# Attention chunks issued in a periodic order written out by hand, on every engine, ahead of a routed feed-forward layer

## The chip, the cores and the metric

One core of a Trainium2 chip. The metric is the device time of one execution in microseconds (us), lower is better. Engines: PE (TensorE: matmuls and transposes, results in PSUM), PEld (its weight loads), DVE (VectorE), ACT (ScalarE), POOL (GpSimd, which also issues some of the DMAs), SP (SyncE, which here only issues DMAs). Each engine runs its instructions in the order of its own queue; an instruction waits there for the semaphores of what it reads, and for its output buffer to be free.

## What is computed

Decayed linear attention in blocks, for 4 batches, 8 heads, 768 positions, 64 channels, and then an expert layer in which every token goes to one of 8 experts of 384 tokens each:

```python
Dmask = where(rel >= 0, lam ** rel, 0)
for b in range(12):                                   # blocks of 64
    intra = einsum('bhic,bhjc->bhij', qb, kb) * Dmask
    intra = einsum('bhij,bhjd->bhid', intra, vb)
    inter = einsum('bhid,bhde->bhie', qb * lam_pow, kv_state)
    out[block] = intra + inter
    kv_state = lam ** 64 * kv_state + einsum('bhsd,bhse->bhde', kb * rev_pow, vb)
x = out as [3072 tokens, 512]
logits = x @ w_gate                                   # [3072, 8]
# greedy in order of falling logits: a token takes its best expert that has room (384 places)
out[mask_e] = relu(x[mask_e] @ w1[e]) @ w2[e]         # e = 0..7
```

## The kernel before

**Attention.** The tokens are worked through in 24 chunks of 128 positions (six to a batch), all 8 heads together. fp32 values are split into a high and a low 16-bit half, and a product is three matmuls (high-high, high-low, low-high). The steps of a chunk g, by the tiles they write (the names stand in the profile's rows and in the program):

- `load`: SP queues `qf`, `kf`, `vf` (256 KB each) from DRAM, three chunks ahead into four buffers.
- `prep`: `kp`, the two halves of k side by side: the high one by ACT (L964), the rest by DVE (L965; called `kpl` below). `vs` = v times a power of lam (POOL, L967), its halves `vh` (ACT, L970) and `vl` (POOL, L972).
- `turn_q`, `turn_k`: PE transposes q and kp (`Tq`, `Tk`, four transposes each); ACT and DVE split q into `qh` and `ql` (L996, L998); ACT copies `kT` (L983).
- `scores`: 24 matmuls into two PSUM banks `S0`, `S1` (`S`, L1009); for each bank ACT copies the high half `sp` (L1014), DVE writes the rest (L1015), POOL masks the triangle (L1018).
- `state`: 12 matmuls add k and v to a running state `stp` (L1068), split into `sth` (ACT) and `stl` (DVE, L1076). It is skipped in a batch's last chunk.
- `inter` and `intra`: the state product (24 matmuls, L1037) and the product with the masked scores (24 matmuls, L1049) add up in the PSUM tile `XL`; DVE scales it to `xs` (L1054). `XL` has one buffer, so a chunk's `inter` can't begin before the last reader of the chunk before is done.
- `turn_x`: SP stores `xs` to `x_dram`; PE transposes it (`Tx`, L1086), ACT and DVE split it into `xh` and `xl` (L1089, L1091).
- `gate`: 12 matmuls (L1105) write the chunk's logits into an unused corner of the **next** chunk's `XL`, and DVE copies them out (L1107). That copy is that tile's last reader.

**Order.** In the attention part a scheduler sets each engine's order from the program text and its own estimates. `run` gives the text: in step s it writes the steps of chunks s - 2 to s + 3 one after another and then calls `hook(s)`, which puts in the router's constants (s = 2), its first steps on logits that are there already (`ranges` in three parts at 19 to 21, `ranks` at 22 to 24: short DVE operations, but for one comparison of 1280 elements in each) and the first nine expert weights (`load_w`, from s = 20).

**Weights.** Each of 16 weights (1 MB in bf16, cast from 2 MB of fp32 on the way) is one DMA in POOL's queue. `load_w` is held back by a one-element DVE copy from a chunk's logits into the weight's tile, which the DMA must wait for.

**Routing and experts** (`_route_and_moe`) follow. There the text's order is kept on PE, POOL and DVE: a chain of short steps finds the places of all tokens; indirect DMAs in POOL's queue gather rows of `x_dram` into `xe`; PE does the two layers (`p`, L611 and L624), ACT copies `hT` and `oe` out of PSUM (`oe` has four buffers), and POOL's indirect DMAs scatter `oe` to the output. The remaining weights are queued between the gathers and scatters.

Of the kernel before, what the change touches and what calls it, by code (L numbers as in the profile page):

```python
# [23 lines left out]
class _Router:  # L24
# [11 lines left out]
    def constants(self):  # L36
# [8 lines left out]

        self.i_kt = iota("i_kt", [P, P, 24], [[1, P], [0, 24]], 1)
        self.i_j = iota("i_j", [P, 29, 24], [[1, 29], [0, 24]], 0)
        self.i_t = iota("i_t", [P, 24, 24], [[0, 24], [128, 24]], 0)
        self.i_p = iota("i_p", [P, 1], [[0, 1]], 0, 1, F32)
        self.i_e = iota("i_e", [P, 8], [[1, 8]], 0, 0, F32)  # L50
        self.i_e1 = iota("i_e1", [P, 8], [[1, 8]], 1, 0, F32)
        self.i_et = iota("i_et", [P, 24, 8], [[0, 24], [1, 8]], -8)
        self.i_g8 = iota("i_g8", [P, 9, 24], [[1, 9], [0, 24]], -8)
        self.gbase = iota("gbase", [1, 9, 24], [[384, 9], [0, 24]], 1, 0, F32)
        i_k = self.i_kt[:, :, 0]
        kvec = []
        for m, sc in enumerate((16384, 128, 1, 4096)):
            kx = rc.tile([P, P], BF16, name=f"kvec{m}")
            V.tensor_scalar(kx, i_k, float(sc), None, OP.mult)
            kvec.append(kx)  # L60
        self.kvec = kvec
        ones = {}
        for sc in (16384, 128, 64, 1):
# [3 lines left out]
        self.ones = ones  # L67
# [3 lines left out]
        slt = rc.tile([P, P], BF16, name="slt")  # L71
        G.memset(slt, 0.0)
        G.affine_select(out=slt, in_=slt, compare_op=OP.is_ge, fill=1.0, base=0,
                        pattern=[[-1, P]], channel_multiplier=1)
        self.slt = slt
        sltm = rc.tile([P, P], BF16, name="sltm")
        V.tensor_scalar(sltm, slt, 1.0, None, OP.subtract)
        self.sltm = sltm
# [19 lines left out]
        G.memset(self.ind2[:, 64:128, :], 0.0)  # L98
# [811 lines left out]
class _Attn:  # L910


    def __init__(self, ctx, tc, q, k, v, lam, w_gate, identf, logits, x_dram):
# [4 lines left out]
        P = 128  # L918
        cp = ctx.enter_context(tc.tile_pool(name="ac", bufs=1))
        self.io = ctx.enter_context(tc.tile_pool(name="aio", bufs=4))  # L920
        self.wk = ctx.enter_context(tc.tile_pool(name="awk", bufs=2))
        self.pt = ctx.enter_context(tc.tile_pool(name="apt", bufs=3, space=bass.MemoryType.PSUM))
        self.p1 = ctx.enter_context(tc.tile_pool(name="ap1", bufs=1, space=bass.MemoryType.PSUM))

        lam_sb = cp.tile([P, 8], F32, name="lam_sb")
        nc.sync.dma_start(out=lam_sb, in_=lam[None, :].to_broadcast([P, 8]))
        n_idx = cp.tile([P, 6], F32, name="n_idx")
        nc.gpsimd.iota(n_idx, pattern=[[P, 6]], base=1, channel_multiplier=1,
                       allow_small_or_imprecise_dtypes=True)
        loglam = cp.tile([P, 8], F32, name="loglam")  # L930
# [4 lines left out]
        lampow = cp.tile([P, 6, 8], F32, name="lampow")  # L935
        lamneg = cp.tile([P, 6, 8], F32, name="lamneg")
        nc.scalar.activation(lamneg, nlog, ACT.Exp, scale=-1.0)  # L937
        nc.scalar.activation(lampow, nlog, ACT.Exp)
        self.lampow, self.lamneg = lampow, lamneg
        wgf = cp.tile([P, 4, 8], F32, name="wgf")  # L940
        nc.sync.dma_start(out=wgf, in_=w_gate.rearrange("(c p) e -> p c e", p=P))
        wgh = cp.tile([P, 4, 8], BF16, name="wgh")
        nc.vector.tensor_copy(wgh, wgf)
        wgl = cp.tile([P, 4, 8], BF16, name="wgl")
        nc.vector.tensor_tensor(wgl, wgf, wgh, OP.subtract)
        self.wgh, self.wgl = wgh, wgl

    def load(self, g):
        nc, P = self.nc, 128
        b, t = divmod(g, 6)  # L950
        ts = slice(t * P, (t + 1) * P)
        qf = self.io.tile([P, 8, 64], F32, tag="qf")
        nc.sync.dma_start(out=qf, in_=self.q[b, :, ts, :].rearrange("h p d -> p h d"))
        kf = self.io.tile([P, 8, 64], F32, tag="kf")
        nc.sync.dma_start(out=kf, in_=self.k[b, :, ts, :].rearrange("h p d -> p h d"))
        vf = self.io.tile([P, 8, 64], F32, tag="vf")
        nc.sync.dma_start(out=vf, in_=self.v[b, :, ts, :].rearrange("h p d -> p h d"))
        return qf, kf, vf

    def prep(self, g, qf, kf, vf):  # L960
        nc, P = self.nc, 128
        t = g % 6
        kp = self.wk.tile([P, 8, 64, 2], F16, tag="kp", bufs=4)
        nc.scalar.copy(kp[:, :, :, 1], kf)  # L964
        nc.vector.tensor_tensor(kp[:, :, :, 0], kf, kp[:, :, :, 1], OP.subtract)  # L965
        vs = self.wk.tile([P, 8, 64], F32, tag="vs")
        nc.gpsimd.tensor_tensor(vs, vf, self.lamneg[:, t, :, None].to_broadcast([P, 8, 64]),  # L967
                                OP.mult)
        vh = self.wk.tile([P, 8, 64], BF16, tag="vh", bufs=5)
        nc.scalar.copy(vh, vs)  # L970
        vl = self.wk.tile([P, 8, 64], BF16, tag="vl", bufs=5)
        nc.gpsimd.tensor_tensor(vl, vs, vh, OP.subtract)  # L972
        d = dict(kp=kp, vh=vh, vl=vl, qf=qf)
        return d

    def turn_k(self, g, d):
        nc, P = self.nc, 128
        kT_ps = self.pt.tile([P, 4, P], F32, tag="T", name="kT_ps")
        kpf = d["kp"].rearrange("p h d s -> p (h d s)").bitcast(F32)
        for hp in range(4):  # L980
            nc.tensor.transpose(kT_ps[:, hp, :], kpf[:, hp * P : (hp + 1) * P], self.identf)  # L981
        kT = self.wk.tile([P, 4, P], F32, tag="kT")
# [4 lines left out]
    def turn_q(self, g, d):  # L987
        nc, P = self.nc, 128
        qf = d["qf"]
        qT_ps = self.pt.tile([P, 4, P], F32, tag="T", name="qT_ps")  # L990
        for hp in range(4):
            nc.tensor.transpose(qT_ps[:, hp, :],  # L992
                                qf[:, 2 * hp : 2 * hp + 2, :].rearrange("p h d -> p (h d)"),
                                self.identf)
        qh = self.wk.tile([P, 4, P], F16, tag="qh", bufs=3)
        nc.scalar.copy(qh, qT_ps)  # L996
        ql = self.wk.tile([P, 4, P], F16, tag="ql", bufs=3)
        nc.vector.tensor_tensor(ql, qT_ps, qh, OP.subtract)  # L998
        d["qh"], d["ql"] = qh, ql

    def scores(self, g, d):
        nc, P = self.nc, 128
        kT, qh, ql = d["kT"], d["qh"], d["ql"]
        S = [self.p1.tile([P, 4, P], F32, tag=f"S{a}", name=f"S{a}") for a in range(2)]
        for hp in range(4):
            for i, (ks, qq) in enumerate(((1, qh), (1, ql), (0, qh))):
# [51 lines left out]
    def state(self, g, d):  # L1058
        nc, P = self.nc, 128
        if g % 6 == 5:  # L1060
            return None
# [75 lines left out]
def kernel(  # L1137
# [23 lines left out]
    with ExitStack() as actx:  # L1161
        attn = _Attn(actx, tc, q, k, v, lam, moe_w_gate, identf, logits, x_dram)

        def hook(s):
            if s == 2:
                router.constants()
# [45 lines left out]
```

## Time and profile before

| | |
|---|---|
| time, median of 3 runs | 325.89 us (323.84 to 327.85) |
| the profiled execution's own time | 328.17 us |
| its span, first to last instruction | 326.4 us |
| mean granted TensorE clock | 0.876 |
| busy share of the span: PE, PEld, DVE, ACT, POOL | 77%, 60%, 58%, 51%, 52% |
| first copy of `kp` (L964), last copy of logits (L1107) | at 6.5 us, at 177.6 to 177.9 us |
| DMA | 52.05 MB moved, mean 159 GB/s |

Times in the rows are us from the span's start. A row of a timeline has start, length, engine, line, operation, output<-inputs, shape, count, and in brackets the idle time before it and what ended it. Busy PE time includes the tail in which a matmul drains, so matmuls that follow closely start more often than their lengths say. The clock column of a stretch is the share of the TensorE clock that was granted.

### The profile page before, as it was taken

Reading aid. Unit: us, or ns where it says so; the run is one execution under the profiler, and the core shown is the slowest. Engines: PE = TensorE matmul, PEld = TensorE weight load, DVE = VectorE, ACT = ScalarE, POOL = GpSimd, SP = SyncE. Lnnn points to the kernel's source line nnn. Section 1 sums busy time; section 2 is a strip of 40 time slices with the busy share of each in tenths; the row PEclk is TensorE's granted clock in tenths of the full one; section 3 lists DMA queues with packets and bytes.
Section 4 is the critical chain, followed back from the end, with each engine's and each line's share of the span. In section 5 each row is a group of like instructions: output and inputs, shape, how many; then the busy total and the mean of one; then the engine's idle time right before and its main releaser. Section 6 shows DMA issues by size and latency. Waiting matters only on the chain.

```text
span 326.4 us, 8813 instructions
## 1 busy us (share of the span) xinstructions
PE 249.9 (77%) x3538; PEld 197.1 (60%) x3551; DVE 190.7 (58%) x597; ACT 167.4 (51%) x297; POOL 169.9 (52%) x189
## 2 busy tenths in 40 slices
PE   1778778777979779788856535899809999899980
PEld 0657657666867668677655424577506666677750
DVE  4568758776696766878987578577705773000000
ACT  3757658676675766766621000255223555556650
POOL 5967646656375563755754708644345217445221
PEclk9999999979797797979895555599967999999996
DMA  8998768866797666973999999999999214434211
GB/s 140 218 166 189 165 151 187 174 140 133 176 194 148 131 137 165 195 155 67 209 222 236 209 209 209 186 204 211 223 224 265 74 66 103 115 94 99 80 69 37
DMA packets 96977, 52.05 MB, mean 159 GB/s; under 512 B 76961, under 2 KB 88225, under 8 KB 96929
## 3 DMA queue, kind: packets, MB, share of 16 engines
q0 software_dynamic: 17920, 26.22, 41.0%
q1 hardware_dynamic: 79008, 25.19, 36.0%
q8 instruction: 30, 0.49, 0.6%
q14 instruction: 19, 0.15, 0.2%
HBM read 58.74 MB, written 12.58 MB: 218 GB/s over the span
## 4 chain that ended last, share of the span: by engine, by line
PE 34%; DVE 20%; POOL 12%; issue 12%; DMA 11%; ACT 8%; SPq 0%; POOLq 0%; DVEq 0%; ACTq 0%
PE p L611 7%; PE p L624 7%; DMA out_dram<-oe,perm 6%; DVE sp L1015 4%; POOL vs L967 4%; ACT sp L1014 4%; DVE xs L1054 4%; POOL sp L1018 4%; DMA xe<-x_dram,perm 4%; PE S L1009 3%; PE XL L1105 2%; PE XL L1049 2%; DVE kp L965 2%; PE kT_ps L981 2%; PE xT_ps L1086 2%
## 5 line engine op out<-in xcount | busy, mean ns | idle before, releaser
L611 PE MATMUL p<-xeT,w 128*128 128x256 bf16 (+1 forms) x512 | 51.7, 255 | 11.5 <-ACT hT L616 8.8
L1018 POOL TENSOR_SCALAR_AFFINE_SELECT sp<-sp 128x512 f32<-128x512 f32 x48 | 36.3, 762 | 44.5 <-DVE sp L1015 35.6
L611 PEld LDWEIGHTS <-w 128*128 128x128 bf16 x512 | 40.1, 100 | 20.0 <-issue 13.6
L630 POOL DMA_INDIRECT out_dram<-oe,perm x24 | 24.1, 1004 | 45.2 <-ACT oe L629 35.7
L624 PE MATMUL p<-w,hT 128*128 128x512 bf16 x179 | 43.3, 379 | 0.8
L1015 DVE TENSOR_TENSOR sp<-S,sp 128x512 bf16<-128x512 f32 x48 | 33.3, 734 | 17.9 <-ACT sp L1014 17.9
L1014 ACT CAST sp<-S 128x512 bf16<-128x512 f32 x48 | 32.5, 739 | 20.8 <-PE S L1009 20.6
L580 POOL DMA_INDIRECT xe<-x_dram,perm x24 | 26.5, 1102 | 31.0 <-DMA w<-in_moe_w_dram 11.4
L616 ACT ACTIVATE hT<-p 128x512 bf16<-128x512 f32 (+1 forms) x64 | 31.3, 491 | 18.9 <-PE p L611 15.1
L972 POOL TENSOR_TENSOR vl<-vs,vh 128x512 bf16<-128x512 f32 x24 | 28.3, 1181 | 13.5 <-ACT vh L970 12.9
L629 ACT COPY oe<-p 128x512 f32<-128x512 f32 x24 | 14.1, 586 | 36.5 <-PE p L624 24.9
L1009 PE MATMUL S<-qh,kT 64*128 64x128 f16 x384 | 30.0, 229 | 1.5 <-DVE sp L1015 1.5
L1049 PE MATMUL XL<-vh,sp 128*128 128x64 bf16 x384 | 24.3, 198 | 7.6 <-POOL sp L1018 7.3
L967 POOL TENSOR_TENSOR vs<-vf,lamneg 128x512 f32<-128x512 f32 x24 | 27.3, 1136 | 3.8 <-ACT lamneg L937 3.8
L598 ACT COPY xeT<-pt 128x1024 bf16<-128x1024 bf16 (+1 forms) x16 | 12.8, 798 | 30.4 <-PE pt L594 30.3
L1049 PEld LDWEIGHTS <-sp 128*128 128x128 bf16 x576 | 21.5, 101 | 10.6 <-POOL sp L1018 9.8
L624 PEld LDWEIGHTS <-hT 128*128 128x128 bf16 x192 | 17.0, 97 | 16.6 <-issue 0.3
L981 PE MATMUL kT_ps<-identf,kp 128*128 128x128 f32 x96 | 18.2, 320 | 9.7 <-DVE kp L965 8.5
L1009 PEld LDWEIGHTS <-kT 64*128 64x128 f16 x576 | 20.4, 99 | 7.0 <-issue 2.3
L1009 PE MATMUL S<-ql,kT 64*128 64x128 f16 x192 | 23.1, 227 | 0.0
L992 PE MATMUL qT_ps<-identf,qf 128*128 128x128 f32 x96 | 18.3, 318 | 5.4 <-DMA qf<-in_q_dram 5.4
L970 ACT CAST vh<-vs 128x512 bf16<-128x512 f32 x24 | 14.9, 620 | 14.4 <-POOL vs L967 14.4
(256 smaller groups left out, 582.9 us busy)
## 6 DMA issues: line engine op xcount, KB each, us to landing
w<-in_moe_w_dram POOLq DMA_DIRECT2D x16, 1024.0 KB, 14.5
qf<-in_q_dram SPq DMA_DIRECT2D x24, 256.0 KB, 3.6
kf<-in_k_dram SPq DMA_DIRECT2D x24, 256.0 KB, 4.6
vf<-in_v_dram SPq DMA_DIRECT2D x24, 256.0 KB, 4.9
x_dram<-xs SPq DMA_DIRECT2D x24, 256.0 KB, 2.2
xe<-x_dram,perm POOLq DMA_INDIRECT x24, 7.0
out_dram<-oe,perm POOLq DMA_INDIRECT x24, 3.3
lam_sb<-in_lam_dram SPq DMA_DIRECT2D x1, 4.0 KB, 2.9
```

What stands on the lines that cost most here:

```text
L580: nc.gpsimd.indirect_dma_start(out=xe[:, c, :], out_offset=None, in_=self.x_dram, in_offset=bass.IndirectOffsetOnAxis(ap=pm, axis=0), boun ...
L611: nc.tensor.matmul(p1[:, f, 0:n, :], self.w1t[e][:, kc, fc * P : (fc + 1) * P], j["xeT"][:, kc, 0:n, :], start=(kc == 0), stop=(kc == 3), ...
L616: nc.scalar.activation(hT[:, fp, :, 0:n, :], p1[:, :, 0:n, :], ACT.Relu)
L624: nc.tensor.matmul(p2, j["hT"][:, kc // 2, kc % 2, c, :], self.w2t[e][:, kc, :], start=(kc == 0), stop=(kc == 7))
L967: nc.gpsimd.tensor_tensor(vs, vf, self.lamneg[:, t, :, None].to_broadcast([P, 8, 64]), OP.mult)
L972: nc.gpsimd.tensor_tensor(vl, vs, vh, OP.subtract)
L981: nc.tensor.transpose(kT_ps[:, hp, :], kpf[:, hp * P : (hp + 1) * P], self.identf)
L1009: nc.tensor.matmul(S[a][:, hp, :], kT[r, hp, :, ks], qq[r, hp, :], start=(i == 0), stop=(i == 2))
L1014: nc.scalar.copy(s[:, :, :, 1], S[a])
L1015: nc.vector.tensor_tensor(s[:, :, :, 0], S[a], s[:, :, :, 1], OP.subtract)
L1018: nc.gpsimd.affine_select(out=sf, in_=sf, compare_op=OP.is_ge, fill=0.0, base=0, pattern=[[0, 4], [1, P]], channel_multiplier=-1)
L1049: nc.tensor.matmul(X[a][:, hp, :], sp[a][:, hp, :, ss], vv[:, h, :], start=(first and hp == 0 and i == 0), stop=(i == 2), skip_group_check ...
```

## The change

The steps of a chunk become methods of their own with the same operations on the same data, but for two: `kpl` moves from DVE to POOL, and the copy `kT` from ACT to DVE. The order of all engines in the attention part is now that of the text (`tc.manual_schedule()`), and the text is made by sorting: operation `name` of chunk g stands at `g * PERIOD + AT[name]`, the router's steps and the weights at numbers of their own. The numbers only sort; nothing waits for a time. A chunk's operations reach over more than four periods, so that in one period S stands for chunk g - 1, G for g - 4, I and X for g - 2, and so on. Names: kph, kpl halves of kp; h0, h1 / l0, l1 / m0, m1 copy, rest and mask of the two score banks; I state product, X score product, G gate, lg its copy, xo the store; lq, lk, lv the loads of chunk g + 4.

```diff
+    PERIOD = 5.30
+    AT = dict(kph=0.00, kpl=0.90, Tq=1.33, vs=2.14, Tk=2.24, qh=3.12, vh=3.74, kT=4.23, ql=4.91,
+              vl=4.98, S=5.82, h1=6.88, h0=7.65, l1=8.00, l0=8.76, m1=8.84, ST=9.08, m0=9.60,
+              sth=11.42, stl=12.39, I=13.36, X=15.17, xs=16.23, Tx=19.16, xh=20.28, xl=22.24,
+              G=23.05, lg=23.70, lq=2.0, lk=2.2, lv=3.4, xo=17.0)
+    AHEAD = 4
...
+    def run(self, others):
+        self.begin()          # lam, then kf before qf and vf, for four chunks
+        work = list(others)
+        work.append((-2.0, self.powers))
+        for g in range(24):
+            for name, at in self.AT.items():
+                t = g * self.PERIOD + at
...
+                work.append((t, lambda f=getattr(self, name), n=g: f(n)))
+        for _, f in sorted(work, key=lambda w: w[0]):
+            f()
...
-        nc.vector.tensor_tensor(kp[:, :, :, 0], kf, kp[:, :, :, 1], OP.subtract)
+        self.nc.gpsimd.tensor_tensor(d["kp"][:, :, :, 0], d["kf"], d["kp"][:, :, :, 1],
+                                     OP.subtract)
...
-        nc.scalar.copy(kT, kT_ps)
+        self.nc.vector.tensor_copy(kT, d["kTp"])
...
-    moe = _Moe(ctx, tc, identb, x_dram, moe_w1, moe_w2, out, 10)
+    moe = _Moe(ctx, tc, identb, x_dram, moe_w1, moe_w2, out, 8)
...
-            for m in {20: (0,), 21: (1, 2), 22: (3,), 23: (4,), 24: (5, 6), 25: (7, 8)}.get(s, ()):
-                moe.load_w(m, logits[0:1, s - 2, 0:1])
+        others = [(t, lambda: next(steps, None))
+                  for t in (-3.0, -1.0, 3.5, 132.3, 135.0)]
+        others += [(t, lambda i=i: router.ranges(logits, 18, attn.ps, "qT", i))
+                   for i, t in enumerate((127.5, 128.0, 128.6))]
+        others += [(t, lambda a=a, b=b: router.ranks(logits, a, b))
+                   for t, a, b in ((129.0, 0, 10), (133.6, 10, 20), (140.9, 20, 23))]
+        others += [(t, lambda m=m: moe.load_w(m)) for m, t in
+                   enumerate((125.3, 126.3, 128.1, 129.0, 130.0, 133.5, 134.0, 134.5))]
+        with tc.manual_schedule():
+            attn.run(others)
...
-    fi = _route_and_moe(ctx, tc, logits, router, moe, range(9, 16))
+    fi = _route_and_moe(ctx, tc, logits, router, moe, range(8, 16))
```

The router's constants become five pieces (the `steps` above), two of them near the end; the clearing of a table (`ind2`) moves from POOL to DVE. The three transposes get PSUM banks of their own (`qT`, `kT`, `xT`, one each) instead of three shared ones; `S0`, `S1`, `XL` and `stp` keep one buffer each. Some SBUF rings change by one buffer (`kp` 4 to 3, `vh` and `vl` 5 to 4, `qh` and `ql` 3 to 4, `sp` 2 to 3, `sth`, `stl`, `xs` 2 to 3).

What this does to the queues, at three places. On PE, where the gate stands, in the middle of attention. Before, the matmuls of L1009 around it are one chunk's scores:

```order
L1009 MATMUL S_852<-qh,kT 128x128
L1105 LDWEIGHTS xh
L1105 MATMUL XL<-wgh,xh 128x8
...
L1105 LDWEIGHTS xl
L1105 MATMUL XL<-wgh,xl 128x8
L1009 LDWEIGHTS kT
L1009 MATMUL S_853<-qh,kT 128x128
```

Now (L1056 scores, L1019 `Tq`, L1182 gate, L1038 `Tk`, L1103 state product, L1159 `Tx`):

```order
L1056 LDWEIGHTS kT
L1056 MATMUL S_866<-qh,kT 128x128
L1019 MATMUL qT_ps<-identf,qf 128x128 x4
L1182 LDWEIGHTS xh
...
L1182 MATMUL XL<-wgh,xl 128x8
L1038 MATMUL kT_ps<-identf,kp 128x128 x4
L1103 LDWEIGHTS qh
...
L1159 MATMUL xT_ps<-identf,xs 128x128 x4
L1114 LDWEIGHTS sp_747
```

The last five score matmuls of a chunk stood behind the gate; now all 24 stand ahead of it, and `Tk`, the state product, `Tx`, the state and the score product of other chunks follow.

On POOL, one chunk's worth in the middle of attention. Before (L967 `vs`, L972 `vl`, AFFINE_SELECT the masks):

```order
L1018 AFFINE_SELECT sp_878<-sp_878 128x512
L967 TENSOR_TENSOR vs<-vf,lamneg 128x512
L1018 AFFINE_SELECT sp_882<-sp_882 128x512
L972 TENSOR_TENSOR vl<-vs,vh 128x512
```

Now:

```order
L996 TENSOR_TENSOR kp<-kf,kp 128x512
L1002 TENSOR_TENSOR vs<-vf,lamneg 128x512
L1083 AFFINE_SELECT sp_592<-sp_592 128x512
L1083 AFFINE_SELECT sp_619<-sp_619 128x512
L1013 TENSOR_TENSOR vl<-vs,vh 128x512
```

A fifth operation, the rest of `kp`, comes in, and the two masks stand together.

On DVE, near the end of attention, behind `ql` of chunk 23 (now; L1141 `stl`, L146 and L159 the first and the long operation of the first `ranks`, L1187 the logits of chunk 20, L1072 the score rests of chunk 23, L1147 `xs`, L1170 `xl`):

```order
L137 TENSOR_SCALAR sc<-sc 128x1
L1141 TENSOR_TENSOR stl<-stp,sth 128x512
L146 TENSOR_REDUCE r_v<-logits 128x10
...
L159 TENSOR_TENSOR ind_160<-q_3581,i_kt 128x128x10
...
L1187 COPY logits<-XL 128x8
L1072 TENSOR_TENSOR sp_3572<-S_3523,sp_3572 128x512
L1072 TENSOR_TENSOR sp_3605<-S_3522,sp_3605 128x512
L1147 TENSOR_TENSOR xs<-XL,lampow 128x2x4x64
L1170 TENSOR_TENSOR xl<-xT_ps,xh 128x512
```

The whole first `ranks` (12 operations) now stands in one piece ahead of the logits of chunk 20 and of the last chunk's score rests, and the second one, likewise, ahead of the logits of chunk 21. On POOL the first weight stands behind `vs` of chunk 23, the others between the last masks, eight in all, none with a copy from the logits ahead of it.

More of the change, by code (lines that the diff above doesn't have):

```diff
@@ L44, in iota @@
             return a
[L46 to L62, printed above, removed]
+        self.ones = ones = {}
         for sc in (16384, 128, 64, 1):
@@ L984, in turn_k, with S @@
         d["kT"] = kT.rearrange("p c j -> p (c j)").bitcast(F16).rearrange(
             "p (c j s) -> p c j s", c=4, s=2)
[L987 to L990, printed above, removed]
+    def S(self, g):
+        d = self.d[g]
+        d["S"] = [self.ps.tile([128, 4, 128], F32, tag=f"S{a}", name=f"S{a}") for a in range(2)]
+        d["sp"] = [None, None]
         for hp in range(4):
[L992 to L999, printed above, removed]
@@ L1044, in intra, with X @@
+    def X(self, g):
+        d = self.d[g]
         first = g % 6 == 0
[L1045 removed]
+        for a in (1, 0):
             for hp in range(4):
                 h = 2 * hp + a
[L1048 to L1051 removed]
```

388 lines of the change are left out of this document (209 added, 179 removed).

## The prediction

> **What bounds the kernel now.** I read the stage table first (one row per stretch of the span: its length, then busy time and instructions of PE, weight loads, DVE, ACT and POOL, the granted clock, the DMA share and GB/s), then the chain of waits inside the first stage, then what PE waits for in the last.
>
> ```profile
> 12.00:143.80 131.80, 105.87 (x1936) 90.33 (x1935) 92.58 (x157) 88.51 (x155) 78.22 (x86) 0.92 0.77 165
> 143.80:177.90 34.10, 24.81 (x481) 20.86 (x480) 30.14 (x87) 16.00 (x28) 19.99 (x23) 0.84 0.93 176
> 177.90:207.10 29.20, 15.14 (x166) 12.89 (x166) 20.77 (x83) 1.01 (x1) 16.05 (x17) 0.50 1.17 209
> 207.10:235.40 28.30, 28.11 (x250) 19.65 (x253) 20.57 (x120) 12.44 (x19) 14.77 (x15) 0.92 1.19 205
> ```
>
> Attention fills the first two stretches; the last logits are copied at 177.9. In the first no engine is full: DVE 70%, ACT 67%, POOL 59%, PE 80% (its drains counted). So order and waits set its pace. The second, with the routing's first steps mixed in, is DVE's (88%). Then come 29.2 us of routing, the experts, a hole of 8.8 us on PE, and the rest of the experts to the span's end at 326.4, 82.2 us.
>
> The chain of waits over one chunk (start, length, what) shows why a chunk takes 7.0 us there (34.89 to 41.90) on idle engines:
>
> ```profile
> 34.89 0.74 ACT sp L1014
> 35.73 0.76 DVE sp L1015
> 36.55 0.64 POOL sp L1018
> 37.19 1.46 POOL vs L967
> 40.41 0.69 DVE xs L1054
> 41.14 0.44 PE XL L1105 x12
> 41.59 0.29 PE S L1009 x5
> 41.90 0.75 ACT sp L1014
> ```
>
> Copy, rest and mask of a chunk's scores, then its product, `xs`, then the gate's 12 matmuls, and only behind these the last five score matmuls of the next chunk, which the next copy needs: a loop from one chunk to the next.
>
> The hole later is a queue:
>
> ```profile
> 222.41 20.56 DMA out_dram<-oe,perm
> 244.21 1.01 PE L611 MATMUL p<-xeT,w 128*128 128x256 bf16 x4 [8.78 <-ACT hT L616]
> ```
>
> An output scatter issued at 222.4 lands at 243.0, behind weights in POOL's DMA queue; ACT's copies wait for its buffer, and PE for ACT.
>
> **The change, part by part.** *The loop.* In the new order all 24 score matmuls stand ahead of the gate, and a chunk's product comes two places later, so the loop above is cut. What can bound a chunk next are the sums of each engine and the remaining loops.
>
> POOL now has, per chunk, `vs`, `vl`, two masks and `kpl` (min/median/max in ns; the last row gives mean ns after its busy time):
>
> ```profile
> L1018 POOL TENSOR_SCALAR_AFFINE_SELECT sp<-sp x48: 624/635/1236, 18.0 to 169.6; 128x512 f32<-128x512 f32 x48
> L967 POOL TENSOR_TENSOR vs<-vf,lamneg x24: 1031/1043/1514, 8.9 to 160.3; 128x512 f32<-128x512 f32 x24
> L972 POOL TENSOR_TENSOR vl<-vs,vh x24: 1146/1158/1698, 12.2 to 167.3; 128x512 bf16<-128x512 f32 x24
> L965 DVE TENSOR_TENSOR kp<-kf,kp x24: 714/766/1216, 7.3 to 158.4; 128x512 f16<-128x512 f32 x24
> L187 POOL TENSOR_TENSOR r_zp<-Z,H 128x192 f16<-128x192 f32 x1 | 0.6, 605 | 0.1
> ```
>
> No row shows `kpl` on POOL. The same subtraction with a dense output, `vl`, took 1.16; the one POOL row with a strided f16 output took 605 ns for 192 elements, 1.61 for 512 if all of it grows. So POOL needs 2 x 0.635 + 1.043 + 1.158 = 3.47, plus 1.16 to 1.61: 4.63 to 5.08 us.
>
> By the Trainium skill (GPSIMD Engine Reference, 4.1 Engine selection) an elementwise operation of two inputs is about 2x slower on GpSimd and belongs on VectorE, which speaks against this move: as an estimate from it, twice the 766 ns is 1.53 and POOL's sum 5.0. The trace's like pair, 1158 against 766, is 1.5x.
>
> DVE back to back starts an operation every 0.59 us, not every 0.68, and its copy of logits is short:
>
> ```profile
> 31.62 0.68 DVE L1091 TENSOR_TENSOR xl<-xT_ps,xh 128x512 bf16<-128x512 f32 x1
> 32.21 0.68 DVE L998 TENSOR_TENSOR ql<-qT_ps,qh 128x512 f16<-128x512 f32 x1
> 34.62 0.17 DVE L1107 COPY logits<-XL 128x8 f32<-128x8 f32 x1 [0.53 <-PE XL L1105]
> ```
>
> DVE gives `kpl` away and takes `kT`: two rests of scores, `kT`, `ql`, `xs`, `xl`, most chunks `stl`, seven starts of 0.6 and 0.17: 4.4 us. ACT loses `kT`. DMA moves the same 1.05 MB a chunk; at 5.1 us a chunk that is 206 GB/s, a share of 0.77 x 206/165 = 0.96, where the rows above reach 1.19; a share of 1.0 is reached at 4.9 a chunk.
>
> The longest loop left runs product, `xs`, `xl`, gate, logits' copy, state product, `Tx`, state, product, since the copy must free the bank for the next chunk. Its PE pieces at full clock, by starts:
>
> ```profile
> 35.04 0.20 PE L1037 MATMUL XL<-sth,qh 64*128 64x64 bf16 x2
> 35.50 0.55 PE L1086 MATMUL xT_ps<-identf,xs 128*128 128x128 f32 x3
> 35.88 0.60 PE L992 MATMUL qT_ps<-identf,qf 128*128 128x128 f32 x4
> 36.31 0.22 PE L1068 MATMUL stp<-vh,kp 128*128 128x128 bf16 x1
> 36.93 0.22 PE L1068 MATMUL stp<-vh,kp 128*128 128x128 bf16 x1
> 112.86 0.71 PE XL L1049 x24
> ```
>
> State product 0.46 (35.04 to 35.50), transposes 0.38 for three, so 0.50 for four, state 0.68 (12 starts, the first and last shown), product 0.71. With `xs` 0.60, `xl` 0.68, gate 0.44, copy 0.17 and some 0.18 of gaps: 4.4 us.
>
> So a chunk costs at least 4.63 (POOL), and 5.08 with the dear `kpl`. POOL and DVE also stretch each other: the `vs` of 1.46 in the chain, 0.42 over its median, lay beside the `kpl` that now leaves DVE. If this stays, 5.08 + 0.42 = 5.5. These sums have no waits, and each of POOL's five operations follows another engine, so I take 5.1, the upper end without stretching; 4.6 and 5.5 stay for the range.
>
> *The start.* `kf` is now queued first:
>
> ```profile
> 2.25 4.23 DMA kf<-in_k_dram
> ```
>
> Issued 1 us earlier, it lets chunk 0 begin at about 5.7 instead of 6.5. 24 chunks of 5.1 end at 128.1.
>
> *The tail.* On DVE `ranges` and the first `ranks` now stand ahead of the logits of chunk 20 and the rests of chunk 23, the second `ranks` ahead of the logits of chunk 21. In the stretch of 87 DVE instructions and 30.14 us above, 35 belong to chunks and 7 are the one-element copies that held the weights back. The new tail keeps 14 of the 35, none of the 7, and adds the mask `sltm`: 30.1 - 21 x 0.6 - 7 x 0.1 + 1.0 + a second `ae` of about 1 = 19 us. Three times DVE then waits for PE with little beside it: a round of state product, `Tx` and product is 0.46 + 0.50 + 0.71 = 1.7 at full clock and 3.0 at half (rows further down); two rounds, the first partly beside chunk 23's rests, and a gate of 0.44 make about 5. The tail is 24 us, and the last logits come at 152.1 instead of 177.9.
>
> *Weights and experts.* The program from routing on is unchanged, except that eight weights are queued ahead instead of nine. Their pace:
>
> ```profile
> 178.39 1.64 POOL L562 DMA_DIRECT2D w<-in_moe_w_dram x2 [1.48 <-DVE r_v L143]
> DMA to landing us min/median/max: 20.6/22.7/24.7
> 202.28 1.77 POOL L562 DMA_DIRECT2D w<-in_moe_w_dram x2
> ```
>
> The two issued at 178.4 and 179.2 land at 199.0 and 203.9, 5 us apart, so the queue was still full when the next two came, 24.4 us after the last logits. Eight queued from 126 (behind chunk 23's `vs`, 5.7 + 23 x 5.1 + 3.2) are through by about 171 (5 to begin, 8 x 5), 19 after the last logits; then the queue runs empty. The next two, at 24.4, find nothing ahead, where they had 1.6 us of weights and four gathers of some 1.8; so they, and the scatters behind them, land about 3.4 sooner counted from the last logits. Routing (29.2) is a chain on DVE and PE and stays; PE's first 28.3 us stay; the hole shrinks to 5.4; 82.2 follow. 145.1 in all.
>
> *Sum.* 152.1 + 145.1 = 297.2 of span, against 326.4. The profiled execution's own time is 328.2, its median of runs 325.9; 29.2 off gives 299.0 for a like execution and **297** for the median.
>
> **The clock.** Rows of 3.41 us, with PE's busy time, instructions and granted clock:
>
> ```profile
> 64.58:68.00 3.42, 1.69 (x42) 1.00 0.40 78
> 68.00:71.41 3.41, 3.41 (x44) 0.50 0.97 237
> 78.24:81.65 3.41, 2.28 (x56) 1.00 0.25 48
> 81.65:85.06 3.41, 3.41 (x38) 0.50 1.04 244
> ```
>
> A row half busy is followed by one at half clock; so is the one of 2.28, two thirds busy. At the present pace PE is busy 80% of the first stretch; with chunks a quarter shorter and the same matmuls it is busy nearly always, and I count no half rows before the tail. The Trainium skill (TensorE: Matmul & The Clock Gate, What's actually happening) wants an idle window of about 3.4 us before the clock halves. Its halves and its window length agree, but 2.28 us busy was enough here, so the trace decides: by the page the clock rival below could not occur, by the rows it can.
>
> **Rivals.** *The clock turns the loop into the bound.* At half clock:
>
> ```profile
> 68.43 0.76 PE XL L1037 x24
> 174.51 0.97 PE xT_ps L1086 x4
> 70.44 1.21 PE stp L1068 x12
> 161.27 1.28 PE XL L1049 x24
> ```
>
> The loop grows by 0.30 + 0.47 + 0.53 + 0.57, and `Tk` (as long as `Tx`), hidden beside the logits' copy at full clock, by some 0.6: 6.9 us a chunk, 297 + 24 x 1.8 = 340. It is slower than before from 6.3 a chunk, that is if three quarters of the rows are halved; it feeds on the waits of a fixed order. Against it: full rows end it.
>
> *The order does not cut the waits*: one late instruction holds its whole engine, and a chunk stays near 6.0 to 6.4, 319 to 328, no change. For it: every engine now waits in order. Against: the loop of the chain is gone by the program.
>
> *POOL is the bound with stretching*, 5.5 a chunk: 307.
>
> **How the numbers follow.** Forecast (4.6 to 5.3 a chunk) 0.65; POOL stretched 0.20; no cut 0.10; clock 0.05. 4.6 a chunk gives 285, 5.5 gives 307; an uncertain 3 in the tail and 3.4 if the hole stays make it 286 to 311, which leaves out about 2 in 10. Two per cent, 319.4 to 332.4, is about what a measurement of this kernel can tell: faster 0.86, same 0.09, slower 0.05.
>
> **What would show it.** `kpl` on POOL between 1.1 and 1.6, masks near 0.64; score copies 5.1 apart; clock 1.00 until about 128; last logits near 152; the hole near 5. I am wrong if POOL idles for DVE or PE in most chunks, if half-clock rows come in mid attention, or if the weights' end moves less than the logits'.

## The result, and the profile after

The changed kernel takes **297.65 us** (median of 4 runs, 296.91 to 299.76); the kernel before, beside it, 326.79 us (4 runs, 323.84 to 327.85). The ratio is 0.913, 95% interval 0.905 to 0.921. The profiled execution took 299.76 us with a span of 298.0; the forecast for a like execution was 299.0 with a span of 297.2.

The stage table of the kernel after, in the columns of the prediction's table (stretch and its length; PE, weight loads, DVE, ACT, POOL busy with their instructions; granted clock; DMA share; GB/s). The stretches are the chunks at their steady pace, the tail to the last logits, the routing, and the experts up to the first hole on PE:

```profile
12.20:119.80 107.60, 102.95 (x2212) 91.31 (x2213) 95.35 (x172) 89.89 (x154) 103.18 (x113) 1.00 0.94 211
119.80:145.50 25.70, 11.51 (x212) 9.94 (x209) 18.03 (x66) 3.84 (x7) 10.86 (x17) 0.68 1.12 207
145.50:175.00 29.50, 15.07 (x167) 12.95 (x167) 20.93 (x83) 1.01 (x1) 14.36 (x16) 0.50 1.00 168
175.00:203.85 28.85, 28.84 (x253) 19.89 (x253) 19.86 (x118) 12.43 (x19) 14.38 (x15) 0.91 1.18 209
```

In the first stretch two engines are now full: POOL is busy 96% of it and PE 96%, at a clock of 1.00. Before, the fullest was PE with 80%.

POOL's timeline over one chunk (start, length, what) shows its five operations without a gap; a row with idle time ahead would end in a bracket. The three lines behind it are from the groups by line, durations of the rest of `kp`, of the masks and of ACT's copies of scores (min/median/max in ns, first and last start):

```profile
50.69 1.04 POOL L1002 TENSOR_TENSOR vs<-vf,lamneg 128x512 f32<-128x512 f32 x1
51.69 1.22 POOL L1083 TENSOR_SCALAR_AFFINE_SELECT sp<-sp 128x512 f32<-128x512 f32 x2
52.88 1.17 POOL L1013 TENSOR_TENSOR vl<-vs,vh 128x512 bf16<-128x512 f32 x1
54.00 1.29 POOL L996 TENSOR_TENSOR kp<-kf,kp 128x512 f16<-128x512 f32 x1
55.22 1.06 POOL L1002 TENSOR_TENSOR vs<-vf,lamneg 128x512 f32<-128x512 f32 x1
```
```profile
L996 POOL TENSOR_TENSOR kp<-kf,kp x24: 1266/1282/1292, 6.3 to 116.3; 128x512 f16<-128x512 f32 x24
L1083 POOL TENSOR_SCALAR_AFFINE_SELECT sp<-sp x48: 628/634/642, 13.8 to 129.3; 128x512 f32<-128x512 f32 x48
L1062 ACT CAST sp<-S x48: 726/748/768, 12.2 to 122.1; 128x512 bf16<-128x512 f32 x48
```

1.282 + 2 x 0.634 + 1.046 + 1.164 = 4.76 us (the last two are the medians of `vs` and `vl`), and the start of the rest of `kp` moves from 6.3 to 116.3 in 23 chunks, 4.78 each. The copies of scores, from the first to the last start in their row over 23 chunks, give 4.78 too (the last is the second of its pair, so this measure, used below as well, is about 0.03 too long). PE is nearly as full: from one state product to the next, two chunks in its timeline,

```profile
51.37 0.20 PE L1103 MATMUL XL<-sth,qh 64*128 64x64 bf16 x2
56.07 0.20 PE L1103 MATMUL XL<-sth,qh 64*128 64x64 bf16 x2
```

lie 4.70 us, and no row of PE between them has idle time ahead. So in a chunk with all its steps POOL's sum and PE's sum are 1% apart. A batch's first chunk has no state product (0.46) and its last no state (0.67), so over all 24 PE's sum is lower, about 4.70 - (0.46 + 0.67) / 6 = 4.5.

The clock by slices of the span, in tenths (the page's line):

```profile
PEclk9999999999999999956555558999697999999996
```

It first falls clearly in slice 18, from about 127 us, behind the last chunks' scores.

The holes on PE among the experts, and the two scatters behind them in the chain of waits:

```profile
211.74 1.01 PE L614 MATMUL p<-xeT,w 128*128 128x256 bf16 x4 [7.89 <-ACT hT L619]
225.38 1.01 PE L614 MATMUL p<-xeT,w 128*128 128x256 bf16 x4 [4.03 <-ACT hT L619]
187.70 17.12 DMA out_dram<-oe,perm
205.70 18.44 DMA out_dram<-oe,perm
```

There are two now, 11.9 us in all, where before there was one of 8.8. The first four scatters need 17 to 21 us to land, and ACT's copies wait for their `oe` buffers.

The span by its parts is 119.8 (5.5 to the first chunk, 24 of 4.76) + 25.7 (tail) + 29.5 (routing) + 28.85 + 7.9 + 9.6 + 4.0 + 72.6 (experts, with the two holes) = 298.0.

### The profile page after: what moved, and what is told of

Same layout as the page of the kernel before. It is cut to its first block, busy times and chain, and to the rows that moved or that the text cites. A ratio compares the mean times of both kernels' runs of the same rounds, so it can differ in the third digit from the quotient of the medians.

```text
span 298.0 us, 8818 instructions
## 1 busy us (share of the span) xinstructions
PE 234.1 (79%) x3551; PEld 186.5 (63%) x3551; DVE 181.3 (61%) x589; ACT 155.3 (52%) x273; POOL 188.0 (63%) x212
## 4 chain that ended last, share of the span: by engine, by line
PE 42%; DMA 20%; POOL 12%; DVE 11%; issue 9%; ACT 3%; SPq 0%; POOLq 0%; ACTq 0%; DVEq 0%
DMA out_dram<-oe,perm 12%; PE p L627 6%; PE p L614 6%; DMA w<-in_moe_w_dram 5%; PE xT_ps L1159 4%; POOL kp L996 4%; PE XL L1114 4%; POOL vl L1013 4%; PE kT_ps L1038 3%; PE stp L1127 3%; PE S L1056 3%; PE XL L1103 3%; PE qT_ps L1019 2%; POOL xe L583 2%; PE XL L1182 2%
## 5 line engine op out<-in xcount | busy, mean ns | idle before, releaser
L614 PE MATMUL p<-xeT,w 128*128 128x256 bf16 (+1 forms) x512 | 53.3, 259 | 14.7 <-ACT hT L619 11.9
L614 PEld LDWEIGHTS <-w 128*128 128x128 bf16 x512 | 40.8, 102 | 24.1 <-issue 17.1
L627 PE MATMUL p<-w,hT 128*128 128x512 bf16 x192 | 45.3, 379 | 0.0
L1072 DVE TENSOR_TENSOR sp<-S,sp 128x512 bf16<-128x512 f32 x48 | 32.9, 741 | 3.6 <-ACT sp L1062 3.6
L1083 POOL TENSOR_SCALAR_AFFINE_SELECT sp<-sp 128x512 f32<-128x512 f32 x48 | 30.1, 635 | 7.9 <-DVE sp L1072 7.1
L996 POOL TENSOR_TENSOR kp<-kf,kp 128x512 f16<-128x512 f32 x24 | 30.7, 1281 | 0.4 <-ACT kp L992 0.4
L1165 ACT CAST xh<-xT_ps 128x512 bf16<-128x512 f32 x24 | 14.2, 592 | 21.4 <-PE xT_ps L1159 20.9
L1002 POOL TENSOR_TENSOR vs<-vf,lamneg 128x512 f32<-128x512 f32 x24 | 25.2, 1048 | 0.1
L1147 DVE TENSOR_TENSOR xs<-XL,lampow 128x512 f32<-128x512 f32 x24 | 16.5, 689 | 13.1 <-PE XL L1114 13.1
L1056 PE MATMUL S<-qh,kT 64*128 64x128 f16 x384 | 22.5, 224 | 1.6 <-DVE kT L1044 1.5
L1114 PE MATMUL XL<-vh,sp 128*128 128x64 bf16 x384 | 22.0, 197 | 0.0
L1056 PEld LDWEIGHTS <-kT 64*128 64x128 f16 x576 | 17.6, 98 | 7.0 <-issue 3.8
L1019 PE MATMUL qT_ps<-identf,qf 128*128 128x128 f32 x96 | 16.6, 299 | 6.4 <-DMA qf<-in_q_dram 6.4
```

The lines of the kernel that those rows point to most:

```text
L614: nc.tensor.matmul(p1[:, f, 0:n, :], self.w1t[e][:, kc, fc * P : (fc + 1) * P], j["xeT"][:, kc, 0:n, :], start=(kc == 0), stop=(kc == 3), ...
L627: nc.tensor.matmul(p2, j["hT"][:, kc // 2, kc % 2, c, :], self.w2t[e][:, kc, :], start=(kc == 0), stop=(kc == 7))
L996: self.nc.gpsimd.tensor_tensor(d["kp"][:, :, :, 0], d["kf"], d["kp"][:, :, :, 1], OP.subtract)
L1002: self.nc.gpsimd.tensor_tensor(d["vs"], d["vf"], self.lamneg[:, g % 6, :, None].to_broadcast([128, 8, 64]), OP.mult)
L1056: self.nc.tensor.matmul(d["S"][a][:, hp, :], d["kT"][r, hp, :, ks], qq[r, hp, :], start=(i == 0), stop=(i == 2))
L1072: self.nc.vector.tensor_tensor(s[:, :, :, 0], self.d[g]["S"][a], s[:, :, :, 1], OP.subtract)
```

## The experiments

Each kernel ran beside the kernel before; the ratios to it carry the comparisons. The changed kernel's is 0.913 (0.905 to 0.921).

**The order without the moves.** `kpl` back on DVE and `kT` back on ACT, every number of the order as it was:

```diff
-        self.nc.gpsimd.tensor_tensor(d["kp"][:, :, :, 0], d["kf"], d["kp"][:, :, :, 1],
+        self.nc.vector.tensor_tensor(d["kp"][:, :, :, 0], d["kf"], d["kp"][:, :, :, 1],
...
-        self.nc.vector.tensor_copy(kT, d["kTp"])
+        self.nc.scalar.copy(kT, d["kTp"])
```

> The new order with the two moves undone: kpl back on DVE, kT back on ACT. Theory (the new order cuts the loop, and a chunk then lasts as long as its longest engine sum): in the kernel after, PE runs its pieces of a chunk back to back in 4.70 us and POOL its five in 4.76. Without kpl POOL has 3.48, DVE 4.3, ACT 4.6, so PE's 4.70 is the longest left: chunks 4.7 to 4.8 apart, 296 to 299 us, no change against after. Rival (the prediction's reason to count kpl on DVE as harmful: POOL and DVE stretch each other, and waits come back): vs near 1.46, chunks 5.1 or more, 305 us or more.

Measured: 315.93 us, ratio 0.970 (0.961 to 0.979). My theory fell; two thirds of the gain are gone. Score copies run from 11.9 to 139.7, 5.56 a chunk. The chain of waits over a chunk shows where:

```profile
80.56 0.71 PE XL L1114 x24
81.33 0.57 issue
81.90 1.42 DVE kp L996
83.32 0.58 DVE xl L1170
83.95 0.41 PE XL L1182 x10
```

Product, `xs` (the "issue" row), then `kpl` of 1.42, then `xl`, then the gate, and PE behind it. On DVE `kpl` stands between `xs` and `xl`, inside the loop from chunk to chunk. That left two readings: the place, or the sharing with POOL that makes it 1.42. The sixth run tells them apart.

**The moves without the order.** The kernel before, `kpl` on POOL and `kT` on DVE, and the scheduler's order:

> The kernel before with the two moves alone (kpl on POOL, kT on DVE), in the scheduler's order. Theory (order is what counts): the loop copy, rest, mask, product, scaling, gate, last score matmuls stays; chunks 6.3 to 6.7 apart, 320 to 328 us, no change. Rival (the relieved DVE and the vanished stretching of POOL carry a good part of the gain): chunks below 6.0, 310 us or less.

Measured: 319.59 us, ratio 0.981 (0.974 to 0.988), a gain of about two per cent. Between the two expectations. Score copies (first and last start in the row) are 6.12 apart, the last copy of logits starts at 164.7 instead of 177.6; but the first gathers then stand behind weights that were queued late, and PE waits for them:

```profile
L1014 ACT CAST sp<-S x48: 727/742/762, 14.0 to 154.8; 128x512 bf16<-128x512 f32 x48
196.94 0.61 PE L594 MATMUL pt<-identb,xe 128*128 128x128 bf16 x4 [5.03 <-DMA xe<-x_dram,perm]
```

So the moves alone give 0.5 us a chunk of 6.65, the order alone, with `kpl` at its number on DVE, 1.1, and both give 1.9: they are not a sum.

**Ten weights queued in attention**, not eight (numbers 135.5 and 136.0 for the new two, six weights left for later):

> The kernel after with ten weights queued during attention instead of eight, the two new ones right behind the others; six instead of eight remain for the queue between gathers and scatters. Theory (the hole on PE comes from the scatters that stand behind late weights, about 5 us for each): the holes of 7.9 and 4.0 us shrink together to some 2 to 4, 289 to 291 us. Rival (the prediction's rule: what counts is when the queue runs empty and what lies ahead of the two weights of the first gathers): the queue is empty 10 us later than before, and the holes stay at about 12 or grow, 297 to 300 us.

Measured: 299.01 us, ratio 0.918 (0.911 to 0.924): no difference from the changed kernel. Both theories were half right. The longest landing of the last five weights, and the waits on PE:

```profile
DMA to landing us min/median/max: 24.2/32.5/40.8
176.29 1.27 PE L597 MATMUL pt<-identb,xe 128*128 128x128 bf16 x8 [3.70 <-DMA xe<-x_dram,perm]
214.68 1.01 PE L614 MATMUL p<-xeT,w 128*128 128x256 bf16 x4 [7.52 <-ACT hT L619]
```

The second hole is gone, 4.0 us, as two weights fewer stand among the scatters. But the tenth weight lands at 175.5 (134.7 + 40.8), the first gathers wait behind it, and PE starts on the experts 3.8 later. The first hole stays; as I read the order of issues, the weights ahead of its scatters are those queued behind the gathers, as many as before.

**The ranks behind the logits' copies:**

```diff
-                   for t, a, b in ((129.0, 0, 10), (133.6, 10, 20), (140.9, 20, 23))]
+                   for t, a, b in ((129.75, 0, 10), (135.05, 10, 20), (140.9, 20, 23))]
```

> The kernel after with the first and the second ranks each moved behind the copy of logits that they stood ahead of (of chunks 20 and 21). Theory (the tail is DVE's work in series with PE's rounds; the ranks of 3.0 and 3.7 us hold back the copy that frees the bank for PE's next round): PE's two rounds of 3.2 us run beside the ranks, the last logits come at about 141 instead of 145.5, 293 us. Rival (DVE's work is full in the tail, so that order within it changes nothing): last logits at 145, 297 us.

Measured: 293.38 us, ratio 0.9025 (0.895 to 0.910), 4.3 us below the changed kernel's median (3.5 by the ratios); the last copy of logits starts at 140.8 instead of 145.3. DVE's rows, of the changed kernel first, then of this one (the first copy of logits, then the two `xs` that wait for PE's rounds):

```profile
127.77 0.16 DVE L1187 COPY logits<-XL 128x8 f32<-128x8 f32 x1
131.17 0.69 DVE L1147 TENSOR_TENSOR xs<-XL,lampow 128x512 f32<-128x512 f32 x1 [1.99 <-PE XL L1114]
139.55 0.69 DVE L1147 TENSOR_TENSOR xs<-XL,lampow 128x512 f32<-128x512 f32 x1 [3.24 <-PE XL L1114]
```
```profile
124.52 0.16 DVE L1187 COPY logits<-XL 128x8 f32<-128x8 f32 x1
128.80 0.68 DVE L1147 TENSOR_TENSOR xs<-XL,lampow 128x512 f32<-128x512 f32 x1
135.01 0.69 DVE L1147 TENSOR_TENSOR xs<-XL,lampow 128x512 f32<-128x512 f32 x1
```

The copy comes 3.2 us sooner and frees `XL`; PE's round runs beside the ranks, and both `xs` find their product done. This is what the theory said, with 141 and 293.

**The later weights behind the scatters**, two at a time:

```diff
-                if later:
-                    moe.load_w(later.pop(0))
                 for c in range(len(jobs[n]["perms"])):
                     yield from moe.down(jobs[n], n % 8, c)
-                    if later and c == 0:
-                        moe.load_w(later.pop(0))
+                for _ in range(2):
+                    if later:
+                        moe.load_w(later.pop(0))
```

> The kernel after, with the weights that are queued between the experts' steps placed two at a time behind an expert's two scatters, not ahead of each. Theory (the holes of 7.9 and 4.0 us are ACT's waits for one of four oe buffers, whose scatters stand behind weights of 5 us each in POOL's queue): the first two scatters have two weights ahead less, land near 199 to 201 instead of 204.8 and 210.5, and the next two near 212; both holes nearly go, 286 to 290 us. Rival (PE waits for the weights' bandwidth, so that any order of the same bytes gives the same): the holes stay near 12, 297 us.

Measured: 292.53 us, ratio 0.896 (0.891 to 0.901), 5.1 us below the changed kernel's median (5.6 by the ratios); the spans of the two profiled executions differ by 7.2. The first two scatters' landings, and what is left of the holes:

```profile
DMA to landing us min/median/max: 12.3/12.7/13.0
213.81 0.60 PE L614 MATMUL p<-xeT,w 128*128 128x256 bf16 x4 [1.63 <-ACT hT L619]
226.39 0.60 PE L614 MATMUL p<-xeT,w 128*128 128x256 bf16 x4 [3.90 <-ACT hT L619]
```

They land 12.3 to 13.0 after issue instead of 17.1 and 20.5. The first hole shrinks from 7.9 to 1.6 us, the second stays (4.0 before, 3.9 now): 5.5 in place of 11.9. The bytes are the same, so the first hole came from the queue's order. I had expected both to go, because I followed only the first four scatters.

**The order alone, with `kpl` ahead of `xs`** (`kT` on ACT; `kph`, which feeds `kpl`, moves with it):

```diff
-AT = dict(kph=0.00, kpl=0.90, Tq=1.33, vs=2.14, Tk=2.24, qh=3.12, vh=3.74, kT=4.23, ql=4.91,
+AT = dict(kph=-1.40, kpl=-0.35, Tq=1.33, vs=2.14, Tk=2.24, qh=3.12, vh=3.74, kT=4.23, ql=4.91,
```

> The new order alone again (kpl on DVE, kT on ACT), but kpl of a chunk moved on DVE from its place between xs and xl to one ahead of xs (and kph on ACT 1.4 earlier in the order's numbers to feed it). In the first run of the order alone the chain ran xs, kpl (1.4), xl, gate: kpl lay inside the loop from chunk to chunk, which then took 5.5. Theory (where an operation stands against the loop decides): DVE is idle ahead of xs for 0.2 to 0.9 us, kpl falls there, chunks 4.8 to 5.1 apart, 299 to 306 us. Rival (kpl on DVE costs through sharing with POOL, wherever it stands; kpl and vs took 2.5 together): chunks stay at 5.4 to 5.6, 313 to 317 us.

Measured: 296.27 us, ratio 0.907 (0.902 to 0.912); against 315.93 with `kpl` one place later on DVE, behind `xs`. Better than either expectation. The busy times of one stretch, 30 to 120 us, of this kernel and then of the changed one (its DVE, ACT and POOL columns third to fifth):

```profile
30.00:120.00 90.00, 87.01 (x1976) 77.88 (x1972) 87.17 (x154) 82.77 (x152) 75.97 (x79) 1.00 0.93 213
30.00:120.00 90.00, 86.47 (x1927) 76.93 (x1924) 81.60 (x149) 75.24 (x129) 86.95 (x95) 1.00 0.90 209
```

Score copies run from 12.6 to 120.0, 4.67 a chunk, with PE and DVE both 97% busy. So `kpl` on DVE costs nothing here when it stands outside the loop; the place was the reason in the first run. The sharing is there too: POOL's `vl` beside it takes 1.62 instead of 1.16, but POOL now has the room.

```profile
66.81 0.78 DVE L996 TENSOR_TENSOR kp<-kf,kp 128x512 f16<-128x512 f32 x1
66.96 1.62 POOL L1013 TENSOR_TENSOR vl<-vs,vh 128x512 bf16<-128x512 f32 x1
```

**Sixteen score matmuls in place of 24** (the product with the low half of q is left out):

```diff
-            for i, (ks, qq) in enumerate(((1, d["qh"]), (1, d["ql"]), (0, d["qh"]))):
+            for i, (ks, qq) in ((0, (1, d["qh"])), (2, (0, d["qh"]))):
```

> The kernel after without the low half of q in the scores (16 matmuls of L1056 in place of 24; the scores lack one of three products), so that PE's pieces of a chunk add up to 4.45 instead of 4.70 us and POOL's stay at 4.76. Theory (POOL's sum is the bound): chunks stay 4.75 to 4.78 apart, 296 to 298 us. Rival (PE, back to back in most chunks, is the bound): chunks 4.5 apart, 291 us.

Measured in one run: 295.71 us. Score copies are 4.76 apart, while PE falls from 86.5 to 82.6 busy in the stretch of 90 us; POOL stays at 87.0:

```profile
L1062 ACT CAST sp<-S x48: 727/746/765, 11.3 to 120.8; 128x512 bf16<-128x512 f32 x48
30.00:120.00 90.00, 82.64 (x1787) 72.90 (x1786) 81.33 (x154) 75.62 (x129) 87.02 (x96) 1.00 0.91 210
```

With less for PE to do the pace does not change. So POOL's sum is the bound of the changed kernel. With POOL relieved, in the sixth run, a chunk took 2% less; whether PE or DVE, both full there, is the next bound was not tested.

**Ranks and later weights together** (the fourth and the fifth edit):

> Both at once: the first and second ranks behind the logits' copies, and the later weights behind the scatters. Theory (two stretches that don't touch, so the gains add up): 4.3 from the tail and 8 to 11 from the holes, 282 to 285 us. Rival (routing is reached sooner, while the eight early weights still go through at the same time, so the first gathers queue behind them): the tail's gain is lost again, 287 to 290 us.

Measured: 288.74 us, ratio 0.884 (0.879 to 0.889): 8.9 below the changed kernel's median. That is 4.3 and 5.1 less 0.5 (by the ratios 3.5, 5.6 and 9.5); they add up. The first expert starts 29.7 behind the start of the last logits' copy (140.7 to 170.4), as in the changed kernel (145.3 to 174.95), so the rival's mechanism is out. The time lies in the rival's range all the same, since the theory had counted 8 to 11 for the holes, where the fifth run had brought 5.1.

**The gate ahead of the scores**, one step moved in the order:

```diff
-          sth=11.42, stl=12.39, I=13.36, X=15.17, xs=16.23, Tx=19.16, xh=20.28, xl=22.24,
-          G=23.05, lg=23.70, lq=2.0, lk=2.2, lv=3.4, xo=17.0)
+          sth=11.42, stl=12.39, I=13.36, X=15.17, xs=16.23, Tx=19.16, xh=20.28, xl=21.60,
+          G=21.70, lg=23.70, lq=2.0, lk=2.2, lv=3.4, xo=17.0)
```

> The kernel after with one step moved: xl and the gate stand earlier in the order (numbers 21.60 and 21.70 instead of 22.24 and 23.05), so that on PE the gate's 12 matmuls stand between a score product and the next scores, as in the kernel before, and no longer behind the scores and Tq. Theory (the gain comes from the gate's place on PE: the scores no longer wait for xs and xl): PE now waits in each chunk from the end of the product for xs (0.6 to 0.7) and xl (0.6), about 1.3 us with the scores queued behind; chunks 5.9 to 6.1 apart, 324 to 329 us. Rival (the deeper overlap of four chunks is what counts, and one gate's place is absorbed by the steps waiting on the other engines): chunks 4.8 to 5.1, 298 to 306 us.

Measured: 333.74 us, ratio 1.015 (1.009 to 1.021): the whole gain is gone. Score copies run from 12.2 to 156.0, 6.25 a chunk. The chain of one chunk:

```profile
67.86 0.71 PE XL L1114 x24
68.63 0.57 issue
69.20 0.69 DVE xl L1170
69.94 0.41 PE XL L1182 x10
70.35 0.78 PE S L1056 x24
71.13 0.59 PE qT_ps L1019 x4
```

From the product's end at 68.57 to the gate PE stands for 1.37 us, while DVE does `xs` and `xl`, and the scores queue behind the gate. Four chunks in flight, `kpl` on POOL, `kT` on DVE, the transposes' own banks and the changed rings are all still there, so without the gate's place they bring nothing; whether the gain needs the banks and rings too, no run tells. A chunk is 0.15 dearer than the upper end expected, and the rows put this down to the clock. By 40 slices of this run, 8.3 us each:

```profile
PEclk9999999899979979797555555599969999999997
```

At full clock the chunks are 5.9 to 6.0 apart from about 28 us on, as expected. But five times before 157 us the clock falls to half for some 3.5 us (0.51 from 57.5 to 61.0), and a chunk there takes 6.5 to 8.2 (7.55 from 57.6 to 65.2). PE was busy for 78% of 20 to 130 us here, 96% in the changed kernel.

**Three edits together**: order alone with `kpl` ahead of `xs`, ranks behind the copies, later weights behind the scatters.

> Three edits together: the order alone with kpl on DVE ahead of xs and kT on ACT, the ranks behind the logits' copies, the later weights behind the scatters. Theory (chunks at PE's 4.67 us, tail and holes as in the runs of each): 1.4 + 4.3 + 5.1 below the kernel after, 286 to 288 us. Rival (DVE, 97% busy with kpl, stretches the tail): 290 us.

Measured: 287.74 us, ratio 0.876 (0.872 to 0.880). As expected, and the lowest ratio, though the eighth and the twelfth run lie within 0.01 of it.

**Ten weights, sooner** (numbers 106 to 130 in place of 125.3 to 136), on top of the three:

> The same three and ten weights queued during attention, from about 17 us earlier on, in places where POOL idles once kpl has left it. Theory (ten queued late cost 3.7 us, since the first gathers lay behind them in the queue, and removed the second hole): queued sooner they are through before the first gathers, the hole left of 3.9 us goes, 281 to 284 us. Rival (weights in the queue during the last chunks slow the loads of q, k and v or hold POOL up): attention ends 2 to 5 us later, 286 to 290 us.

Measured: 312.37 us, ratio 0.951 (0.948 to 0.954). Far worse than the rival. POOL's row says it: `vs` of the last chunk waits 15.3 us for its load of v, which SP issued from 103.2 on, 2.7 us behind the first weight (100.5). The issue itself took 8.2:

```profile
103.22 8.20 SPq L975 DMA_DIRECT2D vf<-in_v_dram  x1
132.68 1.03 POOL L1001 TENSOR_TENSOR vs<-vf,lamneg 128x512 f32<-128x512 f32 x1 [15.32 <-DMA vf<-in_v_dram]
```

**Nine weights, the first right behind the last loads** (numbers 113.5 to 130):

> The run with order, tail and weights, and nine weights queued during attention (seven later), the first at about 106 us, right behind the issue of the last chunk's loads, where the run with ten had queued its first at 100.5 with the last loads still to come, and vs then waited 15.3 us for v. Theory (weights in the queue hurt the loads only if they are queued ahead of them): attention ends as in the run without (last logits near 139), nine weights are through by about 157, when the first gathers come, and one weight less stands among the scatters: 284 to 287 us. Rival (the transfers share the DMA engines with x's stores and the last loads whatever the order): attention ends over 3 us later, 290 us or more.

Measured: 286.53 us, ratio 0.879 (0.874 to 0.884): no difference from the kernel with three edits. Both expectations came in part. The last loads, issued ahead of the first weight (106.1), land after 4.7 to 5.5 us, as the theory said, and from the first expert on the kernel takes 113.0 us instead of 115.8, with one wait of PE above 1 us left, of 2.5. But the last copy of logits starts at 142.3 instead of 138.9. The two DVE rows are one `kpl`, in the run with three edits and then in this one; behind them, this run's hole and last logits:

```profile
107.79 0.90 DVE L995 TENSOR_TENSOR kp<-kf,kp 128x512 f16<-128x512 f32 x1
```
```profile
107.80 3.07 DVE L995 TENSOR_TENSOR kp<-kf,kp 128x512 f16<-128x512 f32 x1
212.32 1.01 PE L614 MATMUL p<-xeT,w 128*128 128x256 bf16 x4 [2.54 <-ACT hT L619]
L1186 DVE COPY logits<-Lo x1: 167/167/167, 142.3 to 142.3; 128x8 f32<-128x8 f32 x1
```

While this `kpl` runs, POOL does `vl` (from 108.3), issues a weight (109.4) and begins `vs` (110.4). `xs` behind it starts 2.0 us later than in the run with three edits, PE stands for most of 110 to 112, and the clock is 0.50 from 114 to 116; the next `xs` is 3.5 late, and that stays to the end. So the rival's mechanism, slow transfers, is not what the rows show: x's stores land after 3.0 to 8.4 us, in the run with three edits after 2.0 to 7.2. Which of POOL's three lengthened `kpl` was not tested. Neither the gain nor the loss can be told from zero in the time.

## Why the prediction was right, and where it was right by luck

The total came within 1 us of the span, but two of its terms were wrong by 7 to 8 us and cancelled. Up to the last logits it forecast 152.1 and 145.5 came; behind them it forecast 145.1 and 152.5 came.

- **The loop is cut: right.** The ninth run puts the gate back between product and scores and returns to 6.0 us a chunk at full clock, 6.25 in the mean. The mechanism that the prediction named is the one that counts.
- **The pace, 5.1 a chunk: 4.78 came.** Its term for POOL was right in kind. `kpl` took 1.28, inside 1.16 to 1.61, and no operation of POOL stretched (`vs` at most 1.07 us, before up to 1.51). The sum is 4.76. What failed was "these sums have no waits ... so I take 5.1": between 30 and 110 us POOL waited 2.1 us in all, for DVE's score rests. With the start, that is 8.3 us too many by the end of the chunks.
- **A sum was missing.** I summed POOL, DVE, DMA and the loop, never PE's pieces: 4.70 us in a full chunk, about 4.5 in the mean. It is below POOL's 4.76, so nothing came of it here.
- **Start 5.7: 5.5 came.**
- **The tail, 24 us: 25.7 came.** DVE's work was sized 19 and took 18.0; its waits for PE were sized 5, and it stood idle for 7.7. The fourth run, with the last logits 4.5 sooner, shows what of it comes from the place of the ranks.
- **Routing 29.2 and PE's first 28.3: 29.5 and 28.85 came.**
- **The hole shrinks to 5.4: 11.9 came.** This step failed. The early weights are through at 165.6 (133.3 + 32.3 in the last one's issue and landing), 20 us after the last logits where 19 were forecast, and the queue does run empty. But the two weights of 169.8 and 170.7 gained nothing by it. Landing after issue, min/median/max of these two, in the kernel after and then in the kernel before:

```profile
DMA to landing us min/median/max: 9.7/12.2/14.6
DMA to landing us min/median/max: 10.4/12.4/14.5
```

The sum let the first of them land 3.4 us sooner, after 7.0 in place of 10.4; it took 9.7. The very first weight of all, with none ahead of it, took 9.2. So what lay ahead cost 0.7 and not 3.4, and the first hole fell from 8.8 to 7.9 only. And I passed over what eight in place of nine means: one weight more in the queue among the scatters, and a second hole of 4.0. The third run takes two from there and removes the second hole; the fifth sets them behind the scatters and nearly removes the first.

- **The rivals.** The clock stayed at 1.00 to 122.8 us, so the rival of the loop at half clock met none of its conditions; in the ninth run, where the order leaves PE waiting in each chunk, half clock did come in mid attention. POOL did not stretch. "The order does not cut the waits" was nearer than 0.10 says: `kpl` at its number on DVE makes 5.56 a chunk, the gate 1.4 numbers earlier 6.25, slower than before. I judged the order as one thing; a wrong place for either of two steps takes away two thirds of the gain or all of it.
- **`kpl` on POOL.** The Trainium skill (GPSIMD Engine Reference, 4.1 Engine selection) puts an elementwise operation of two inputs at about twice its time on VectorE; here it was 1.28 against 0.77, 1.7 times. It sends such work to VectorE, and the sixth run does so, at 296.27 against 297.65 us, no difference that the intervals can tell: the move is not what gained, given a place on DVE outside the loop.

## What to carry to other kernels

When order is written by hand, look first for the chain that closes from one iteration to the next, and ask of each operation on its engines whether it stands inside that loop: a gate moved by two places cost 33 us here by the ratios, and a subtraction moved by one was worth 20. Add up every engine's work for one iteration, the matmul engine's too; where the loop was shorter than the largest sum, that sum came without a margin for waits. In a queue that carries both large loads and small stores that something waits for, count what stands ahead of each small one; a total that comes out right does not show that its terms are.

## What the runs showed of the hardware

- A subtraction on DVE with both inputs in SBUF (`kpl`) and an operation on POOL lengthen each other: in the first run `kpl` took 1.42 (0.77 at the median before), in the sixth `vl` on POOL 1.62 instead of 1.16, and in the twelfth one `kpl` took 3.07 beside `vl`, a weight's issue and `vs`. DVE's other subtractions read one input from PSUM, and in the changed kernel's attention, without `kpl` on DVE, none of POOL's five takes over 1.3 us. The Trainium skill (SBUF — State Buffer, Who interferes with whom) says that a DVE instruction with two SBUF inputs contends with a GpSimd one that reads SBUF. The rows agree.
- The loads in SP's queue suffer from weights queued earlier in POOL's: a load of 256 KB took up to 29.4 us to land in the eleventh run, 4.3 to 5.2 in the tenth and 4.7 to 5.5 in the twelfth, where no weight was ahead of it.
- Short waits of PE were enough for half clock. In the ninth run no single wait of PE between 30 and 150 us is above 1.4 us, and from 20 to 130 us PE is busy 78%; the clock still fell to half five times before 157 us. In the changed kernel, with PE busy 96% from 12 to 120 us, it stayed at 1.00.
